# First expert chosen from summed slot values, the second batch's keys and values ahead of W1, one subtraction on GpSimd, and W1's product split in halves

## The chip, the cores and the metric

The kernel runs on one core of a Trainium2 chip. The metric is the device time of one execution in microseconds; the number that counts is the median of three executions.

## The reference

Two layers follow each other. The first is a Linformer-like attention for 8 batches, 8 heads, 576 tokens, head size 64 and 32 memory slots; the second is a mixture of 8 experts in which every token goes to one expert.

```python
a = softmax(phi, axis=2)                        # over the 576 tokens, for each of the 32 slots
k_m = einsum('bhsm,bhsd->bhmd', a, k)           # 32 keys per head
v_m = einsum('bhsm,bhsd->bhmd', a, v)           # 32 values per head
x = softmax(q @ k_m.T / 8) @ v_m                # tokens x (8 heads * 64)
xn, en = x / |x|, expert_emb / |expert_emb|     # router
expert = argmax(xn @ en.T / tau); gate = max(softmax(xn @ en.T / tau))
out = gate * (relu(x @ w1[expert]) @ w2[expert])
```

## The kernel before

**Layout.** The 8 heads are two groups `g` of four, so that 4 heads by 32 slots fill 128 partitions. All matrices are float32. The product with W1 is folded into the values: `project` multiplies the 32 slot values of every head with the head's rows of W1 (tile `pg`), and `first` then multiplies the attention weights of the tokens with that product (tile `ph`). Both operands of `ph` are cut into a rounded part and a rest: `aT[0]` and `aT[1]` for the weights (`part`), `gh` (ScalarE) and `gl` (VectorE) for the product. `ph` has three matmuls per group, of which the third needs `gl`.

**Order.** Nothing is scheduled by the compiler: every engine runs its instructions in the order in which the Python code emits them, and semaphores make it wait for data and for free buffers. PSUM has eight tiles by tag, `m0` to `m3` (taken in turn by `mm`, or by number) and `t0` to `t3` (`pt`). A new tile in a tag waits until the last reader of the old one is done. In particular `pg` of group 0 and the first tile `ph` both lie in `m0`, and `pg` of group 1 and the second `ph` in `m1`; the tile `tv` of the second batch's values and the first tile `tt` of `turned` both lie in `m2`. DMAs of the SP queue have eight completion semaphores in turn, so the ninth waits for the first.

**The start.** The change is in the start of the program alone, up to the first `ph`. It runs through batch 0's softmax over tokens (`softmax`, `turn`, `tails`: exponentials `ex`, transposed into `eT`), the slot sums (`slots`, into `ks`), keys and values (`keys`, `values`: tiles `tk`, `tv`, copied to `kT`, `vT`), the scores (`score`: tiles `tr` and `te`, turned into `x` by `fill`), the softmax over slots (`weigh`: maximum, subtraction, exponential; `divide`: sum, reciprocal, product; `turn`: into `aw`), the attended values and router logits (`attend`: tile `po`, then `best`), and the transposes of `turned` (tile `tt`). The same first steps for batch 1 are interleaved. Every batch's tokens take mainly one expert, whose weights are loaded whole; for batch 0 the kernel guesses this expert early (`guess`, `pick`) so that the load of W1 can start. Before the change the guess sums `vv[:, g, D : D + E]`, the logits of every slot, which `squares` (tile `tl`) and `products` have to make first. `warm` issues matmuls whose results nobody reads.

From the first `ph` on (L759) the TensorE works through `first` and `second` of batch 0, the next batches' steps laid between, to the end.

Of the kernel before, what the change touches and what calls it, by code (L numbers as in the profile page):

```python
# [8 lines left out]
F32 = mybir.dt.float32  # L9
# [4 lines left out]
ALU = mybir.AluOpType  # L14
AX = mybir.AxisListType
# [12 lines left out]
BL = S // 32  # L28
HS = S // 2
# [18 lines left out]
class Tokens:  # L48
# [15 lines left out]
        for g in gs:  # L64
            nc.vector.transpose(k.x[:, g, ks], src[g])

    def weigh(self, gs, ks):
        k, nc, b = self.k, self.nc, self.b
        x = k.x[:, gs[0] : gs[-1] + 1, ks]
        n = len(gs) * (ks.stop - ks.start)  # L70
        mx = k.wk.tile([P, *x.shape[1:3]], F32, tag=f"mx{n}", name=f"mx{b}_{gs[0]}{ks.start}")
        nc.vector.tensor_reduce(out=mx, in_=x, axis=AX.X, op=ALU.max)
        yield
        nc.vector.tensor_tensor(out=x, in0=x, in1=mx.unsqueeze(3).broadcast_to(x.shape), op=ALU.subtract)
        yield
        nc.scalar.activation(x, x, AF.Exp, scale=1.0 / 8.0)

    def divide(self, gs, ks, apart=False):
# [8 lines left out]
        nc.vector.reciprocal(out=z, in_=z)  # L87
        for i in parts:
# [94 lines left out]
    def all_at_once(self):  # L183
# [4 lines left out]
        nc.vector.tensor_reduce(out=key, in_=self.room.rearrange("p (i e) -> p e i", e=E), axis=AX.X, op=ALU.add)  # L188
        return key

    def guess(self):

        k, nc = self.k, self.nc
        key = self.pt([P, 512], "key")
        self.spare, self.key = key[:, E:], key[:, :E]
# [89 lines left out]
class Kernel:  # L285
# [312 lines left out]
    def keys(self, b, room=None):  # L598

        ts = [(room or self.pt)([P, NG, P], f"tk{b}_{g}") for g in range(1 if b else NG)]  # L600
        for g in range(NG):
            self.nc.tensor.transpose(ts[-g][:, g], self.ks[:, g, : 2 * D], self.ident)
        kT = self.kT[b % 2]
        if b > 1:
            self.nc.vector.tensor_copy(kT, ts[0])
        elif b:
            self.nc.scalar.copy(kT, ts[0])
        else:
            self.nc.scalar.copy(kT[:, 0], ts[0][:, 0])
            self.nc.vector.tensor_copy(kT[:, 1], ts[1][:, 1])  # L610

    def by_feature(self, b):

# [114 lines left out]
    def project(self, n, vT, room=None, apart=False):  # L728

        nc = self.nc  # L730
        for k in range(2):
            f = slice(512 * k, 512 * k + 512)
            ps = [(room or self.mm)([P, 512], f"pg{n}_{k}{g}") for g in range(NG)]
            for g, j, r, c, i in self.heads():
                nc.tensor.matmul(ps[g][j], lhsT=vT[r, g, c % 2, i], rhs=self.w1s[r, c, f], start=True, stop=True)
            if apart and not k:
                yield
            for g in range(NG):
                nc.scalar.copy(self.gh[:, g, f], ps[g])  # L739
            if apart and not k:  # L740
                yield
            for g in range(NG):
                nc.vector.tensor_tensor(  # L743
                    out=self.gl[:, g, f], in0=ps[g], in1=self.gh[:, g, f].bitcast(F32), op=ALU.subtract
                )
            yield

# [183 lines left out]
    def batch(self, b, t, u):  # L931
# [150 lines left out]
def moe_linformer(ctx, tc, phiT, qT, kv, kvt, emb, tau, w1, w2, out):  # L1082
    k = Kernel(ctx, tc, phiT, qT, kv, kvt, emb, tau, w1, w2, out)
# [42 lines left out]
    def scores(g):  # L1126
        k.score(0, tr, 64, S, (g,))
        k.score(0, te, 0, 64, (g,))

    scores(0)  # L1130
# [5 lines left out]
    scores(1)
    work = [t.weigh((g,), all) for g in range(NG)]
    t.fill((0,), slice(2, BL), tr)
    t.fill((0,), slice(0, 2), te)
    e = t.pick()  # L1140
# [5 lines left out]
    list(work[0])  # L1146
    for g in range(NG):
        k.largest(1, g)
        k.softmax(1, (g,))
    k.turn(1, 0)  # L1150
    k.warm(2, at=2)
    t.fill((1,), slice(2, BL), tr)
    t.fill((1,), slice(0, 2), te)
    list(work[1])
# [4 lines left out]
    next(project)  # L1159
# [3 lines left out]
    t.divide(range(NG), all, True)  # L1163
    k.invert(1)
    next(project)
    k.scale(1)
    k.again(k.nc.scalar.copy)
    t.turn(range(NG), all)
    next(project)
    k.part(0, slice(0, HS), k.nc.scalar.copy)  # L1170
    k.keys(1, lambda *a: k.mm(*a, 3))
    k.values(1, copy=k.nc.scalar.copy, room=lambda *a: k.mm(*a, 2))
    k.part(1, slice(0, HS), k.nc.scalar.copy)
    k.load_w2(e)
# [37 lines left out]
```

## Time and profile before

| what | value |
|---|---|
| median of 3 runs | 394.56 us (394.25 to 394.57) |
| the profiled execution's own time | 397.13 us |
| its span, first to last instruction | 395.3 us |
| PE busy | 384.2 us, 97% of the span |
| DVE, ACT, POOL busy | 243.5, 213.8, 188.0 us |
| DMA moved | 91.25 MB, mean 231 GB/s |

Busy time is the time in which an engine had an instruction running. The profiled execution took 1.8 us more than its span, and 2.6 us more than the median of the runs.

### The profile page before, as it was taken

To read this page: it belongs to the slowest core of one execution; us is meant where nothing else is said; L and a number is where in the kernel's file an instruction comes from. 1 tells how busy PE (TensorE), PEld (TensorE's weight loads), DVE (VectorE), ACT (ScalarE), POOL (GpSimd) and SP (SyncE) were. 2 spreads that over 40 slices of the span, in tenths; PEclk is the share of its full clock that TensorE was granted. 3 is DMA by queue.
4 is the path that set the end of the run, shared out by engine and by line. 5 is a ranking of instruction groups with operands and counts; after the bars stand their busy time and mean duration, and the time that the engine had idled before them with its cause. 6 is when DMAs were issued, how large, how long until landed. Compare 5 with 4: busy or idle time off the path is not lost. (4 is left out here: it accounts for less than half of the span.)

```text
span 395.3 us, 10409 instructions
## 1 busy us (share of the span) xinstructions
PE 384.2 (97%) x3886; PEld 314.1 (79%) x3886; DVE 243.5 (62%) x799; ACT 213.8 (54%) x666; POOL 188.0 (48%) x231
## 2 busy tenths in 40 slices
PE   8869999999999999999999999999999999999995
PEld 5547978879787987879787897879788897879883
DVE  5485896768872798538971698627961596545000
ACT  5257652868675685657665775667632651145011
POOL 1034971479142951559142971549342781529300
PEclk9989999999999999999999999999999999999999
DMA  7999907898679926997479945997269305890011
GB/s 262 388 335 376 380 29 155 293 384 332 153 218 390 396 80 148 328 375 308 77 167 385 378 163 108 343 373 283 57 158 393 142 2 103 247 397 2 30 53 43
DMA packets 67751, 91.25 MB, mean 231 GB/s; under 512 B 40968, under 2 KB 45576, under 8 KB 67568
## 3 DMA queue, kind: packets, MB, share of 16 engines
q1 hardware_dynamic: 64320, 81.02, 61.5%
q0 software_dynamic: 2688, 8.26, 5.8%
q10 hardware_dynamic: 688, 1.26, 1.1%
q8 instruction: 32, 0.52, 0.6%
q14 instruction: 23, 0.19, 0.2%
HBM read 71.19 MB, written 19.33 MB: 229 GB/s over the span
## 5 line engine op out<-in xcount | busy, mean ns | idle before, releaser
L759 PE MATMUL ph<-aT,gh 128*128 128x288 f32 x512 | 103.1, 297 | 0.0
L799 PE MATMUL py<-wh,hh 128*128 128x512 f32 x256 | 100.9, 394 | 0.0
L799 PE MATMUL py<-wh,hl 128*128 128x512 f32 x256 | 99.9, 390 | 0.0
L799 PE MATMUL py<-wl,hh 128*128 128x512 f32 x256 | 99.9, 390 | 0.0
L725 POOL TENSOR_TENSOR wl<-w2s,wh 128x512 fp32r<-128x512 f32 x64 | 83.1, 1299 | 5.1
L759 PEld LDWEIGHTS ph<-aT,gh 128*128 128x128 f32 x512 | 81.8, 188 | 1.8 <-DVE hl L766 0.8
L759 PE MATMUL ph<-aT,gl 128*128 128x288 f32 x256 | 75.5, 295 | 0.0
L763 ACT ACTIVATE hh<-ph 128x224 fp32r<-128x224 f32 (+1 forms) x128 | 48.8, 388 | 33.7 <-PE ph L759 33.0
L766 DVE SCALAR_TENSOR_TENSOR hl<-ph,hh 128x224 fp32r<-128x224 f32 (+1 forms) x128 | 51.9, 417 | 23.9 <-ACT hh L763 17.2
L804 ACT ACTIVATE ys<-py,gate 128x512 f32<-128x512 f32 (+1 forms) x40 | 25.7, 643 | 62.8 <-PE py L799 33.0
L968 POOL DMA_DIRECT2D out_dram<-ys x28 | 16.2, 580 | 90.0 <-ACT ys L804 89.9
L799 PEld LDWEIGHTS py<-wh,hh 128*128 128x128 f32 x256 | 48.2, 188 | 11.0 <-issue 1.4
L799 PEld LDWEIGHTS py<-wh,hl 128*128 128x128 f32 x256 | 48.1, 188 | 10.1
L799 PEld LDWEIGHTS py<-wl,hh 128*128 128x128 f32 x256 | 48.1, 188 | 9.4
L759 PEld LDWEIGHTS ph<-aT,gl 128*128 128x128 f32 x256 | 48.1, 188 | 0.0
L743 DVE TENSOR_TENSOR gl<-pg,gh 128x512 fp32r<-128x512 f32 x32 | 20.0, 684 | 42.3 <-ACT gh L739 42.3
L715 POOL TENSOR_TENSOR aT<-aw,aT 128x576 fp32r<-128x576 f32 (+1 forms) x18 | 23.5, 1318 | 37.6 <-DVE aT L714 29.3
L724 POOL CAST wh<-w2s 128x512 fp32r<-128x512 f32 x62 | 41.2, 665 | 0.1
L554 ACT COPY eT<-xt 32x256 f32<-32x256 f32 x80 | 32.3, 404 | 1.4
L788 PE MATMUL py<-w2s,h 128*64 128x256 f32 x256 | 29.4, 383 | 0.0
L626 ACT COPY kv<-kt 32x64 f32<-32x64 f32 x96 | 23.3, 243 | 6.4 <-DVE kt L616 5.2
L788 PEld LDWEIGHTS py<-w2s,h 128*64 128x64 f32 x256 | 17.7, 137 | 10.7 <-DVE aw L100 2.1
(176 smaller groups left out, 474.6 us busy)
## 6 DMA issues: line engine op xcount, KB each, us to landing
kx<-kv SPq DMA_DIRECT2D x32, 512.0 KB, 10.4
w2s<-w SPq DMA_DIRECT2D x28, 512.0 KB, 9.9
w1s<-w SPq DMA_DIRECT2D x28, 512.0 KB, 6.3
qt<-qT SPq DMA_DIRECT2D x14, 576.0 KB, 9.1
out_dram<-ys POOLq DMA_DIRECT2D x28, 256.0 KB, 6.3
ad<-aw SPq DMA_DIRECT2D x8, 576.0 KB, 11.1
td<-x SPq DMA_DIRECT2D x56, 72.0 KB, 2.4
ea<-td SPq DMA_DIRECT2D x7, 512.0 KB, 4.2
```

The source lines that it names most:

```text
L554: nc.scalar.copy(eT[to, :8, m].rearrange("p (g k) m -> p g k m", g=NG), xt[at, :, q : BL - 2 : 4])
L626: nc.scalar.copy(y, self.kt[32 * l : 32 * l + 32, g, h + 2 * i :: 2 - 4 * i])
L715: self.nc.gpsimd.tensor_tensor(out=al, in0=a, in1=ah.bitcast(F32), op=ALU.subtract)
L724: (copy or self.nc.scalar.copy)(h, x)
L725: self.nc.gpsimd.tensor_tensor(out=l, in0=x, in1=h.bitcast(F32), op=ALU.subtract)
L743: nc.vector.tensor_tensor(out=self.gl[:, g, f], in0=ps[g], in1=self.gh[:, g, f].bitcast(F32), op=ALU.subtract)
L759: nc.tensor.matmul(p, lhsT=w[:, g, fs], rhs=x[:, g, to], start=g == 0 and k == 0, stop=g == 1 and k == 2)
L763: nc.scalar.activation(self.hh[:, f, at], q, AF.Relu)
L766: nc.vector.scalar_tensor_tensor(out=self.hl[:, f, at], in0=q, scalar=0.0, in1=self.hh[:, f, at].bitcast(F32), op0=ALU.max, op1=ALU.subtract)
L788: nc.tensor.matmul(p[64 * j : 64 * j + 64], lhsT=self.h4[:, f], rhs=self.w2s[:, f, d * j : d * j + d], start=f == 0, stop=f == 7,)
L799: nc.tensor.matmul(p, lhsT=h[:, f, to], rhs=w[:, f], start=f == 0 and k == 0, stop=f == 7 and k == 2)
L804: nc.scalar.activation(y[:, :d], p, AF.Copy, scale=gate[:, i : i + 1])
```

## The change

The key of the first guess is made from the slot sums directly: `summed` multiplies `ks` with `fours` (a column of ones for each head's 32 slots), which gives the sum of the values over slots, and VectorE multiplies it with the embeddings (`ve`); `guess` then sums over partitions. The transposes of the values (`tv`) move behind the first group's scores. On the SP queue all four tiles `kx` of batch 1 stand ahead of W1 (before: three, then W1's first half, then the fourth), and the second half of batch 0's queries goes behind the first half of batch 1's phi. The subtraction of `weigh` for group 0 runs on GpSimd. Batch 1's slot sums move ahead of `project`; `again` for batch 1 moves from ScalarE to GpSimd; `gh` and `gl` of W1's first half are made in column halves, and `gl` moves behind `attend`. The warm matmuls in the middle go from 42 of 168 columns to 26 of 128, and from 2 of 512 columns to 3.

```diff
-    def weigh(self, gs, ks):
+    def weigh(self, gs, ks, v=None):
...
-        nc.vector.tensor_tensor(out=x, in0=x, in1=mx.unsqueeze(3).broadcast_to(x.shape), op=ALU.subtract)
+        (v or nc.vector).tensor_tensor(out=x, in0=x, in1=mx.unsqueeze(3).broadcast_to(x.shape), op=ALU.subtract)
...
+    def summed(self):
+        k, nc = self.k, self.nc
+        self.key = self.pt([P, 512], "key")
+        self.vs = vs = self.key[:, 508:].rearrange("p (g k) -> p g k", g=NG)
+        for g in range(NG):
+            for h in range(2):
+                nc.tensor.matmul(
+                    vs[64 * h : 64 * h + 64, g],
+                    lhsT=k.ks[:, g, D * (1 - h) : D * (2 - h)],
+                    rhs=k.fours[:, h ^ g :: 2],
+                    start=True,
+                    stop=True,
+                )
+        self.ve = k.wk.tile([P, NC, E], F32, tag="ve", name="ve")
+        x = self.ve.rearrange("p (g k) e -> p g k e", g=NG)
+        em = k.vT[1][:, :, 0, D:].rearrange("p g (k e) -> p g k e", e=E)
+        nc.vector.tensor_tensor(out=x, in0=em, in1=vs.unsqueeze(3).broadcast_to(x.shape), op=ALU.mult)
...
-        for g in range(NG):
-            nc.tensor.matmul(self.key, lhsT=k.all1, rhs=k.vv[:, g, D : D + E], start=not g, stop=g == NG - 1)
+        for c in range(NC):
+            nc.tensor.matmul(self.key, lhsT=k.all1, rhs=self.ve[:, c], start=not c, stop=c == NC - 1)
...
-            for g in range(NG):
-                nc.scalar.copy(self.gh[:, g, f], ps[g])
+            n = 2 if apart and not k else 1
+            for j, g in ((j, g) for j in range(n) for g in range(NG)):
+                to, at = slice(512 // n * j, 512 // n * (j + 1)), slice(512 * k + 512 // n * j, 512 * k + 512 // n * (j + 1))
+                nc.scalar.copy(self.gh[:, g, at], ps[g][:, to])
...
-    k.load_q(0)
+    k.load_q(0, (0,))
...
-    k.load_phi(1)
+    k.load_phi(1, (0,))
+    k.load_q(0, (1,))
+    k.load_phi(1, (1,))
...
+    k.load_kv(1)
+    k.keys(0)
+    t.summed()
     k.again()
-    k.load_kv(1, (0, 1, 2))
-    k.keys(0)
-    k.values(0, copy=k.nc.scalar.copy)
...
-    k.load_w1(e, 0)
-    k.load_kv(1, (3,))
-    k.load_w1(e, 1)
-    k.load_q(1, (0,))
-    k.warm(42, hot=t.spare[:, :168])
...
+    k.softmax(1, (0,))
+    list(work[0])
+    k.warm(26, hot=k.mm([P, 128], "warm", 3))
+    k.turn(1, 0)
+    k.softmax(1, (1,))
+    k.warm(3, at=3)
     k.turn(1, 1)
     k.tails(1)
+    list(work[1])
     k.shares(1, v=k.nc.gpsimd, invert=False)
...
     for ks in ((0,), (1,), (4,), (2,), (3,)):
         k.slots(1, accs, ks=ks, first=0 in ks, last=3 in ks)
+    t.divide(range(NG), all, True, lambda: k.invert(1))
...
+    k.scale(1)
+    k.keys(1, lambda *a: k.mm(*a, 3))
+    k.again(k.nc.gpsimd.tensor_copy)
+    values = k.values(1, copy=k.nc.scalar.copy, room=lambda *a: k.mm(*a, 2))
+    next(values)
+    t.turn((0,), all)
+    k.part(0, slice(0, HS), k.nc.scalar.copy)
     next(project)
+    t.turn((1,), all)
     next(project)
     k.part(1, slice(0, HS), k.nc.scalar.copy)
+    t.attend()
+    next(project)
+    list(values)
+    t.turned(0, 1)
+    t.turned(4)
```

On TensorE, between batch 1's slot sums (`acc0t`, `acc`) and the attended values (`po`), the program has this before:

```order
L577 MATMUL acc0t<-kx_73,eT 32x128 x4
L577 MATMUL acc0m<-kx_73,eT 32x128 x4
L602 MATMUL tk_0_544<-ident,ks 128x128 x2
L637 MATMUL tv_0_548<-ident,ks 128x128 x2
L131 MATMUL po_0_569<-vv,aw 64x72
```

And this after:

```order
L601 MATMUL acc0t<-kx_73,eT 32x128 x4
L601 MATMUL acc_469<-kx_73,eT 32x128 x4
L626 MATMUL tk_0_520<-ident,ks 128x128 x2
L661 MATMUL tv_0_525<-ident,ks 128x128 x2
L760 MATMUL pg_00_532<-w1s,kv_80 32x512 x4
L760 MATMUL pg_01_533<-w1s,kv_80 32x512 x4
L133 MATMUL po_0_550<-vv,aw 64x72
```

W1's product `pg`, which stood ahead of all slot sums of batch 1, now stands behind them, between the values and `po`.

On ScalarE, the two exponentials of batch 1's phi (`ex`), the two exponentials of batch 0's scores (`x`) and the copies of the transposes (`eT`, `kt`) stand before in this order:

```order
L76 ACTIVATE x<-x 128x576
L494 ACTIVATE ex,sm_435<-ex,nm_434 128x576 x2
L521 COPY eT<-te_0_443 128x512
L76 ACTIVATE x<-x 128x576
L521 COPY eT<-te_1_458 128x512
L528 COPY kt<-tz_464 128x256
```

And after in this one:

```order
L518 ACTIVATE ex,sm_401<-ex,nm_400 128x576
L76 ACTIVATE x<-x 128x576
L545 COPY eT<-te_0_438 128x512
L518 ACTIVATE ex,sm_401<-ex,nm_400 128x576
L545 COPY eT<-te_1_450 128x512
L552 COPY kt<-tz_456 128x256
L76 ACTIVATE x<-x 128x576
```

Phi's second exponential now stands behind the first copy, and the second exponential of the scores behind all copies.

On VectorE, from the last transposes into `aw` to the rests `gl`, the program has before:

```order
L98 STREAM_TRANSPOSE aw<-x 128x576
L100 STREAM_TRANSPOSE aw<-x 128x64
L743 TENSOR_TENSOR gl<-pg_00_473,gh 128x512
L743 TENSOR_TENSOR gl<-pg_01_474,gh 128x512
L145 TENSOR_REDUCE lg_255<-po_0_569 128x24
```

And after:

```order
L100 STREAM_TRANSPOSE aw<-x 128x576
L102 STREAM_TRANSPOSE aw<-x 128x64
L147 TENSOR_REDUCE lg_257<-po_0_550 128x24
L147 TENSOR_REDUCE l_594<-po_1_551 128x24
L147 TENSOR_REDUCE lg_257<-po_2_552 128x16
L147 TENSOR_REDUCE l_594<-po_3_553 128x16
L148 TENSOR_TENSOR lg_257<-lg_257,l_594 128x40
L156 TENSOR_REDUCE m_260<-lg_257 128x5
L157 TENSOR_TENSOR oh_175<-lg_257,m_260 128x40
L771 TENSOR_TENSOR gl<-pg_00_532,gh 128x256
L771 TENSOR_TENSOR gl<-pg_01_533,gh 128x256
```

The rests `gl` move behind the seven instructions that turn `po` into the choice of experts.

## Rows read from the trace of the kernel before

**Rows 1.** The page, part 1: busy us (share of the span) x instructions, by engine.

```profile
PE 384.2 (97%) x3886; PEld 314.1 (79%) x3886; DVE 243.5 (62%) x799; ACT 213.8 (54%) x666; POOL 188.0 (48%) x231
```

**Rows 2.** Stretches: length, busy us per engine, granted clock, DMA share, GB/s.

```profile
13.00:19.00 6.00, 5.17 (x80) 2.90 (x73) 3.19 (x11) 2.31 (x10) 0.00 (x0) 1.00 1.03 411
19.00:22.00 3.00, 3.00 (x42) 2.99 (x40) 2.96 (x6) 2.31 (x5) 0.29 (x2) 1.00 0.68 222
23.20:26.20 3.00, 0.00 (x0) 0.00 (x0) 2.81 (x7) 1.43 (x3) 1.37 (x5) 0.93 0.97 322
26.20:29.20 3.00, 2.98 (x40) 1.25 (x44) 2.11 (x5) 0.98 (x2) 0.92 (x1) 0.50 1.05 410
...
34.30:391.00 356.70, 356.29 (x3441) 295.06 (x3439) 223.34 (x735) 197.59 (x623) 181.21 (x210) 1.00 0.67 223
```

**Rows 3.** TensorE in order of time: start, length, instruction, what ended idle time.

```profile
14.68 1.06 PE L655 MATMUL tr<-qt,kv 64*32 64x512 f32 x8
...
16.53 0.85 PE L197 MATMUL key<-vv,h 128*128 128x8 f32 x4 [0.47 <-ACT vv L701]
17.32 1.06 PE L655 MATMUL tr<-qt,kv 64*32 64x512 f32 x8
...
18.42 3.22 PE L417 MATMUL key<-ones 128*128 128x168 bf16 x42
21.48 0.60 PE L520 MATMUL te<-ident,ex 128*128 128x128 f32 x4
...
26.22 1.96 PE L735 MATMUL pg<-w1s,kv 64*32 64x512 f32 x16 [3.05 <-DMA w1s<-w]
...
31.60 0.44 PE L602 MATMUL tk<-ident,ks 128*128 128x128 f32 x2 [0.56 <-ACT ks L594]
...
32.30 1.48 PE L131 MATMUL po<-vv,aw 64*64 64x72 f32 x80
...
34.34 0.51 PE L759 MATMUL ph<-aT,gh 128*128 128x288 f32 x2
...
36.10 1.09 PE L735 MATMUL pg<-w1s,kv 64*32 64x512 f32 x16
```

**Rows 4.** ScalarE in order of time, same columns.

```profile
14.78 0.90 ACT L642 COPY kv<-tv 64x64 f32<-64x64 f32 x4 [0.41 <-PE tv L637]
...
20.27 0.78 ACT L494 ACTIVATE ex<-ex,nm 128x576 f32<-128x576 f32 x1
...
22.17 0.59 ACT L521 COPY eT<-te 128x512 f32<-128x512 f32 x1 [0.28 <-PE te L520]
23.21 0.68 ACT L76 ACTIVATE x<-x 128x576 f32<-128x576 f32 x1 [0.45 <-DVE x L74]
...
24.27 0.38 ACT L528 COPY kt<-tz 128x256 f32<-128x256 f32 x1
...
28.22 1.07 ACT L739 CAST gh<-pg 128x512 fp32r<-128x512 f32 x2 [3.58 <-PE pg L735]
```

**Rows 5.** VectorE in order of time, same columns.

```profile
18.76 0.76 DVE L74 TENSOR_TENSOR x<-x,mx 128x576 f32<-128x576 f32 x1
...
28.83 1.29 DVE L743 TENSOR_TENSOR gl<-pg,gh 128x512 fp32r<-128x512 f32 x2 [0.78 <-ACT gh L739]
...
34.18 0.48 DVE L146 TENSOR_TENSOR lg<-lg,l 128x40 f32<-128x40 f32 x1
...
34.93 0.20 DVE L155 TENSOR_TENSOR oh<-lg,m 128x40 bf16<-128x40 f32 x1
...
54.60 1.70 DVE L74 TENSOR_TENSOR x<-x,mx 128x576 f32<-128x576 f32 x1
```

**Rows 6.** GpSimd in order of time, same columns.

```profile
5.49 0.24 POOL L496 COPY xt<-ex 128x64 f32<-128x64 f32 x1 [3.72 <-ACT ex L494]
...
25.48 1.63 POOL L90 TENSOR_TENSOR x<-x,z 128x576 f32<-128x576 f32 x1 [1.45 <-DVE z L87]
...
53.16 2.52 POOL L725 TENSOR_TENSOR wl<-w2s,wh 128x512 fp32r<-128x512 f32 x2
```

More of the change, by code (lines that the diff above doesn't have):

```diff
@@ L73, in weigh, with divide @@
         yield
-        nc.vector.tensor_tensor(out=x, in0=x, in1=mx.unsqueeze(3).broadcast_to(x.shape), op=ALU.subtract)
+        (v or nc.vector).tensor_tensor(out=x, in0=x, in1=mx.unsqueeze(3).broadcast_to(x.shape), op=ALU.subtract)
         yield
         nc.scalar.activation(x, x, AF.Exp, scale=1.0 / 8.0)
-    def divide(self, gs, ks, apart=False):
+    def divide(self, gs, ks, apart=False, then=None):
         k, nc, b = self.k, self.nc, self.b
@@ L87, in divide @@
         nc.vector.reciprocal(out=z, in_=z)
+        if then:
+            then()
         for i in parts:
@@ L189, in all_at_once @@
         return key
+    def summed(self):
[15 more added lines that the diff above has]
+        nc.vector.tensor_tensor(out=x, in0=em, in1=vs.unsqueeze(3).broadcast_to(x.shape), op=ALU.mult)
     def guess(self):
         k, nc = self.k, self.nc
-        key = self.pt([P, 512], "key")
-        self.spare, self.key = key[:, E:], key[:, :E]
-        for g in range(NG):
-            nc.tensor.matmul(self.key, lhsT=k.all1, rhs=k.vv[:, g, D : D + E], start=not g, stop=g == NG - 1)
+        self.key = self.key[:, :E]
+        for c in range(NC):
+            nc.tensor.matmul(self.key, lhsT=k.all1, rhs=self.ve[:, c], start=not c, stop=c == NC - 1)
     def pick(self):
@@ L366, in consts @@
         nc.gpsimd.memset(self.all1, 1.0)
+        self.fours = st([P, 4], F32, name="fours")
+        nc.vector.tensor_reduce(
+            out=self.fours, in_=self.ident.rearrange("p (m x) -> p m x", m=4), axis=AX.X, op=ALU.add
+        )
         self.half = st([P, 1], F32, name="half")
@@ L608, in keys @@
         else:
-            self.nc.scalar.copy(kT[:, 0], ts[0][:, 0])
-            self.nc.vector.tensor_copy(kT[:, 1], ts[1][:, 1])
+            for g in range(NG):
+                self.nc.scalar.copy(kT[:, g], ts[g][:, g])
     def by_feature(self, b):
@@ L737, in project @@
                 yield
-            for g in range(NG):
-                nc.scalar.copy(self.gh[:, g, f], ps[g])
+            n = 2 if apart and not k else 1
+            for j, g in ((j, g) for j in range(n) for g in range(NG)):
+                to, at = slice(512 // n * j, 512 // n * (j + 1)), slice(512 * k + 512 // n * j, 512 * k + 512 // n * (j + 1))
+                nc.scalar.copy(self.gh[:, g, at], ps[g][:, to])
             if apart and not k:
                 yield
-            for g in range(NG):
+            for j, g in ((j, g) for j in range(n) for g in range(NG)):
+                to, at = slice(512 // n * j, 512 // n * (j + 1)), slice(512 * k + 512 // n * j, 512 * k + 512 // n * (j + 1))
                 nc.vector.tensor_tensor(
-                    out=self.gl[:, g, f], in0=ps[g], in1=self.gh[:, g, f].bitcast(F32), op=ALU.subtract
+                    out=self.gl[:, g, at], in0=ps[g][:, to], in1=self.gh[:, g, at].bitcast(F32), op=ALU.subtract
                 )
@@ L1119, in moe_linformer @@
     k.scale(0)
+    k.load_kv(1)
+    k.keys(0)
+    t.summed()
     k.again()
-    k.load_kv(1, (0, 1, 2))
-    k.keys(0)
-    k.values(0, copy=k.nc.scalar.copy)
+    values = k.values(0, copy=k.nc.scalar.copy, room=lambda *a: k.mm(*a, 3))
     all, tr, te = slice(0, BL), [k.mm([P, S - 64], f"tr0_{g}", g) for g in range(NG)], [k.mm([P, 64], "te0_0", 2)]
[L1126 to L1130, printed above, removed]
+    k.score(0, tr, 64, S, (0,))
@@ L1131, in moe_linformer @@
+    t.guess()
+    k.score(0, te, 0, 64, (0,))
+    next(values)
+    t.fill((0,), slice(2, BL), tr)
+    e = t.pick()
+    t.fill((0,), slice(0, 2), te)
+    list(values)
+    k.load_w1(e, 0)
+    k.load_w1(e, 1)
+    k.load_q(1, (0,))
     tl = [k.pt([P, D + E], f"tl0_{g}") for g in range(NG)]
     k.squares(0, tl)
+    k.score(0, tr, 64, S, (1,))
+    te.append(k.pt([P, 64], "te0_1"))
+    k.score(0, te, 0, 64, (1,))
     k.products(0, copy=True)
-    t.guess()
-    te.append(k.pt([P, 64], "te0_1"))
@@ L1136, in moe_linformer @@
[L1136 to L1140, printed above, removed]
-    k.load_w1(e, 0)
-    k.load_kv(1, (3,))
-    k.load_w1(e, 1)
-    k.load_q(1, (0,))
-    k.warm(42, hot=t.spare[:, :168])
-    list(work[0])
+    work = [t.weigh((g,), all, None if g else k.nc.gpsimd) for g in range(NG)]
+    next(work[0])
     for g in range(NG):
         k.largest(1, g)
-        k.softmax(1, (g,))
-    k.turn(1, 0)
-    k.warm(2, at=2)
+    next(work[0])
@@ L1152, in moe_linformer @@
     t.fill((1,), slice(2, BL), tr)
     t.fill((1,), slice(0, 2), te)
-    list(work[1])
+    k.softmax(1, (0,))
[4 more added lines that the diff above has]
+    k.warm(3, at=3)
     k.turn(1, 1)
     k.tails(1)
+    list(work[1])
     k.shares(1, v=k.nc.gpsimd, invert=False)
     project = k.project(0, k.vT[0], apart=True)
-    next(project)
+    accs = [accs[0], k.mm([P, 2 * D], "acc1", 3)]
     for ks in ((0,), (1,), (4,), (2,), (3,)):
@@ L1161, in moe_linformer @@
         k.slots(1, accs, ks=ks, first=0 in ks, last=3 in ks)
+    t.divide(range(NG), all, True, lambda: k.invert(1))
     k.tags, k.turns = 4, 3
-    t.divide(range(NG), all, True)
-    k.invert(1)
+    k.scale(1)
+    k.keys(1, lambda *a: k.mm(*a, 3))
+    k.again(k.nc.gpsimd.tensor_copy)
+    values = k.values(1, copy=k.nc.scalar.copy, room=lambda *a: k.mm(*a, 2))
+    next(values)
+    t.turn((0,), all)
+    k.part(0, slice(0, HS), k.nc.scalar.copy)
     next(project)
-    k.scale(1)
-    k.again(k.nc.scalar.copy)
@@ L1168, in moe_linformer @@
-    t.turn(range(NG), all)
+    t.turn((1,), all)
     next(project)
-    k.part(0, slice(0, HS), k.nc.scalar.copy)
-    k.keys(1, lambda *a: k.mm(*a, 3))
-    k.values(1, copy=k.nc.scalar.copy, room=lambda *a: k.mm(*a, 2))
     k.part(1, slice(0, HS), k.nc.scalar.copy)
+    t.attend()
+    next(project)
+    list(values)
+    t.turned(0, 1)
+    t.turned(4)
     k.load_w2(e)
```

4 lines of the change are left out of this document (1 added, 3 removed).

## The prediction

> **What bounds the kernel now.** I read the page first: TensorE is busy for 97% of the span [rows 1]. The table of stretches then says where it is not: from 34.3 us on, where `ph` starts, it is busy for 356.29 of 356.70 us [rows 2]. Nothing behind 34.3 us waits to be shortened, so the change can only move the moment at which this solid block begins. A start earlier by so much ends the kernel earlier by so much, as long as nothing later runs out of data.
>
> The timeline of TensorE shows what holds that moment back [rows 3]. The last transposes of batch 0's side work start at 21.48 us, and then nothing until 26.22 us, when `pg` starts with 3.05 us of idle time before it, ended by the DMA of W1. Two things come on top. The table of stretches shows the DMA at 411 GB/s up to 19 us but at 222 GB/s from 19 to 22 us: the queue ran dry there, waiting for the expert's choice [rows 2]. And the granted clock, still 0.93 on average over the idle stretch, is 0.50 over 26.2 to 29.2 us, that is 1.2 instead of 2.4 GHz [rows 2]: the first `pg` takes 1.96 us where the second, at full clock, takes 1.09 [rows 3]. From there one thing follows the other: slot sums, `tk` at 31.60, `po` at 32.30, `ph` at 34.34 [rows 3].
>
> **The change part by part.** All times below are moments in the span, to be held against 34.34 for the first `ph`.
>
> *DMA and W1.* Ahead of W1 now stands another tile `kx` of 512 KB, 1.3 us at 411 GB/s. Before, 189 GB/s were lost for 3 us, some 570 KB [rows 2]; that hole closes, since W1 is asked for while the queue is still full. So W1's first half lands about as before, between 25 and 27 us (from 26.22). But `pg` now stands behind the slot sums and values and comes to it only near 29 us (below). W1 is off the path with 2 us to spare, and so is the moment of the guess; the price of the extra tile is nothing, and 1.3 us if that cover were gone. The second half of W1 and W2 keep their order and move the same way.
>
> *Up to the second group's scores.* Batch 0's keys come as before. In place of the two transposes of the values stand eight passes of `key` (four matmuls, two passes each) with 64-column weights. The nearest row is the old `key`: four passes in 0.85 us, a wait in between included [rows 3], so 0.2 us each at most. They hide partly behind the copy of `kT`; I take the first scores `tr` at 14.7 instead of 14.68, at worst 15.4. Behind `tr` (0.9 us from start to the next start) come the new `guess`, eight passes with 128-column weights: between 0.85 (the old four with no wait) and 1.7 us; I take 1.1, since one of the two starts in the old row was a wait. Then the transposes `tv`, their four copies on ScalarE (0.90 us [rows 4]) and `tl`. That puts the second `tr` at 18.1 us, against 17.32 [rows 3]: later by 0.8.
>
> *The warm matmuls.* From `tr` to the warm ones it is 1.1 us (17.32 to 18.42). The old 42 took 3.22 us [rows 3]; 26 of 128 columns instead of 168 are 3.22 x 26/42 x 128/168 = 1.5 us. So the transposes `te` of phi start at 18.1 + 1.1 + 1.5 = 20.7 us, 0.8 earlier than 21.48.
>
> *GpSimd's subtraction.* VectorE's took 0.76 us [rows 5]; the nearest row on GpSimd, a product of the same shape, took 1.63 [rows 6]. It runs beside VectorE's two maxima of phi, from about 18.5 to 20.2 us. The exponential that reads it must be done before the copy of `te` at 21.4, so it is hidden with 0.5 us to spare. What may break this cover is contention: an identical subtraction on VectorE, beside GpSimd's `wl`, took 1.70 instead of 0.76 us [rows 5, 6]; doubled, GpSimd's would take 3.3 and cost 1.1 us. The Trainium skill (GPSIMD Engine Reference, section Specifications) says that the two engines share their SBUF interfaces and get in each other's way when VectorE's instruction reads two tensors from SBUF. Maxima read one, so by that rule the subtraction stays near 1.6 and the sum is as mine; the slow row of 1.70 us agrees, as that subtraction reads two.
>
> *ScalarE's new order.* Here the change costs. `te` at 20.7 gives its copy at 21.4 (0.69 later, as 21.48 to 22.17 [rows 3, 4]), done at 22.0. Only then comes phi's second exponential, 0.78 us [rows 4], with its accumulator about 22.9; then the second `te`, whose copy runs from 23.6 to 24.2, the tail's copy (0.38) to 24.5, and the second exponential of the scores, 0.68 us, to 25.1. Before, that ended at 23.21 + 0.68 = 23.89 [rows 4]. So `weigh` ends 1.2 us later, and it now stands on the path.
>
> *The slot sums* start at about 23.6 and end near 26.3 us, at full clock: no idle stretch of 3 us stands before them any more. They would be done 4 us earlier than before, but their scaling waits for the reciprocals that VectorE makes behind the sums of `divide`.
>
> *From `divide` to `po`.* From the end of that exponential to the end of GpSimd's product it took 27.11 - 23.89 = 3.2 us [rows 4, 6]; the instructions between are the same, so the product ends at 28.3. Behind it on GpSimd stands `again`: 128 columns, where 64 took 0.24 us [rows 6], so between 0.24 and 0.5; I take 0.3. The transposes `tv` wait for it and `pg` waits behind them, so `pg` runs from 28.9 to 29.9 (1.02 to the next start, at full clock), and `po` starts at 29.95, 2.35 us earlier than 32.30. `aw`, ready at 29.3, is in time.
>
> *From `po` to `ph`.* The choice of experts ended 35.13 - 32.30 = 2.8 us after `po` began [rows 3, 5], of which 0.48 was one sum of 40 columns, where the maximum's flags of the same size took 0.20 [rows 5]; I take 2.7, that is 32.65. Only now come the four halves of `gl`. The old two took 1.29 us [rows 5]; a half costs between 0.32 (half of 0.65) and 0.65; I take 0.36. The first `ph` writes to the tag `m0`, which the third half is the last to read, so it starts after three of them, 1.1 us, at 33.75. Before, `gl` was done long ahead; this is 1.1 us given back. ScalarE's four half casts (the old two took 1.07 [rows 4]) and its copies of `tv`, on which `tt` waits, end near 32.7 and hide behind `po` and `gl`.
>
> *The sum.* 34.34 - 33.75 = **0.6 us earlier**. The gain of 2.35 us at `po` comes from the wait for W1 and the halved clock; `gl`, the later start of `po`'s reader and the longer chain on ScalarE give the rest back. The span goes from 395.3 to 394.7 us. The profiled execution was 2.6 us above the median, so I subtract from the median: 394.56 - 0.6 = 394.0 us.
>
> **The rivals.** A run of this kernel varies by 0.3 us, and 0.2%, 0.8 us, is about what can be told from no change; below 393.8 is faster, above 395.35 slower.
>
> *The chain is shorter than I add it up* (18%). The bounds of `guess` (0.25 us down), `gl` (0.1) and the choice of experts (0.2 down, if that sum takes 0.20), and an earlier first copy on ScalarE, together give 0.6 to 1.5 us more: 393.0 us. For it speaks that `po` moves by 2.35 us, against it that all of this lies in series on three engines.
>
> *The clock falls* (15%). This one ends slower. Before, three idle microseconds were followed by the granted clock 0.50 [rows 2]. After the change no gap is that long, but between 22 and 33 us there are idle stretches of 1.0, 0.5, 0.9, 0.9 and 1.3 us by the sums above. If the clock is 0.50 when `pg` and `po` run, `pg` takes 1.96 for 1.09 [rows 3] and `po` up to 2.9 for 1.48: 1.8 to 2.3 us more, against 0.6 gained. The point of decision is whether the clock is at 1.2 GHz at 29 us; time 395.7 us. The Trainium skill (TensorE: Matmul & The Clock Gate, section What's actually happening) says that the slow clock is the default and activity lifts it; sparse work would then cost it, which rows 2 bear out for an empty stretch only.
>
> *Nothing is gained* (12%): the first scores start late (15.4), or the second exponential does by another 0.7 us; then `ph` starts at 34.4 and the time is 394.6 us.
>
> *W1 is late after all:* it would have to land after 28.9 us, 2.7 later than now, with less than 1.3 us of transfer added. I give it nothing of its own.
>
> **How the numbers follow.** My own case has 55%, with 393.4 to 394.6 as its range, a third of it below 393.8. Faster: 0.20 from it and 0.18 from the shorter chain, 0.38. Slower: 0.14 from the clock and 0.03 from the lost gain, 0.17. The same: 0.45. The range reaches from the shorter chain to the slow clock, 392.9 to 395.6 us.
>
> **What the profile will show.** Right: no wait for W1 ahead of `pg`; DMA near 400 GB/s from 19 to 22 us; the second exponential of the scores ending near 25 us; `tv` waiting for GpSimd's `again`; `po` near 30; the first `ph` near 33.75, with a wait for `gl` before it. Wrong: a granted clock of 0.50 behind 26 us; `pg` waiting for a DMA; a subtraction on GpSimd of over 2 us; TensorE idle anywhere behind the first `ph`.

## The result, and the profile after

The changed kernel takes 398.22 us (median of 22 runs, 396.85 to 402.74), the kernel before, run beside it, 396.33 us (22 runs, 393.86 to 399.23). The ratio is 1.0058, with a 95% interval of 1.0033 to 1.0083. I forecast 394.0 us, a gain of 0.6; by the ratio the change costs about 2.3 us (the two medians lie 1.9 us apart).

The profiled execution of the changed kernel took 401.59 us. The stretches of its span (length, busy us of each engine, granted clock, DMA share, GB/s) answer to [rows 2]:

```profile
19.00:22.00 3.00, 2.71 (x29) 1.57 (x30) 2.52 (x6) 2.06 (x9) 1.16 (x1) 0.50 0.80 308
14.20:24.30 10.10, 9.81 (x81) 6.05 (x81) 5.27 (x14) 3.61 (x13) 1.40 (x2) 0.50 0.96 370
...
38.50:395.00 356.50, 356.50 (x3438) 294.87 (x3438) 222.80 (x733) 196.48 (x620) 180.89 (x209) 1.00 0.67 219
```

The second row shows a granted clock of 0.50, that is 1.2 GHz, for 10 us, in the middle of the steps whose lengths I had added up at 2.4 GHz. In the kernel before, it was 0.50 at another place, over 26.2 to 29.2 us [rows 2]. TensorE in order of time, against [rows 3]:

```profile
14.91 1.93 PE L680 MATMUL tr<-qt,kv 64*32 64x512 f32 x8
16.78 1.88 PE L217 MATMUL key<-ve,h 128*128 128x8 f32 x8
...
25.07 0.61 PE L544 MATMUL te<-ident,ex 128*128 128x128 f32 x4
...
33.24 1.09 PE L760 MATMUL pg<-w1s,kv 64*32 64x512 f32 x16
34.26 1.48 PE L133 MATMUL po<-vv,aw 64*64 64x72 f32 x80
36.69 0.87 PE L165 MATMUL tt<-ident,aw 128*128 128x128 f32 x6 [0.94 <-ACT kv L667]
38.42 0.50 PE L787 MATMUL ph<-aT,gh 128*128 128x288 f32 x2 [0.86 <-DVE gl L771]
```

`tr` takes 1.93 us here, where it took 1.06 at full clock, and everything behind it is late: `ph` starts at 38.42 us, not at the 33.75 of the forecast. But this is one execution of 22, slower than the median by 3.4 us, so a bad clock in it alone can't be the reason of the median. Two questions follow: does the chain come out as forecast when the clock stays up, and if it does, why is the kernel slower?

Each run carries the mean granted clock of its span. A run whose profile shows a fall of 3.4 us ahead of the end has 0.995 or less (the profiled execution of before: 0.995). Below, a run is called *clean* when its mean is 0.996 or more. The limit is a rough one: nine of the 54 clean runs of the kernel before stand at 0.996 exactly, with a median of 396.9 us, so some of them may hold a fall.

### The profile page after: what moved, and what is told of

The parts are those of the page before. It is cut to its first block, busy times and chain, and to the rows that moved or that the text cites. A ratio compares the mean times of both kernels' runs of the same rounds, so it can differ in the third digit from the quotient of the medians.

```text
span 399.8 us, 10412 instructions
## 1 busy us (share of the span) xinstructions
PE 387.5 (97%) x3883; PEld 315.1 (79%) x3883; DVE 243.2 (61%) x801; ACT 213.7 (53%) x668; POOL 188.9 (47%) x233
## 3 DMA queue, kind: packets, MB, share of 16 engines
q10 hardware_dynamic: 688, 1.26, 1.1%
## 5 line engine op out<-in xcount | busy, mean ns | idle before, releaser
L771 DVE TENSOR_TENSOR gl<-pg,gh 128x512 fp32r<-128x512 f32 (+1 forms) x34 | 20.1, 651 | 42.8 <-ACT gh L766 42.8
L740 POOL TENSOR_TENSOR aT<-aw,aT 128x576 fp32r<-128x576 f32 (+1 forms) x18 | 23.5, 1318 | 35.9 <-DVE aT L739 29.2
## 6 DMA issues: line engine op xcount, KB each, us to landing
w2s<-w SPq DMA_DIRECT2D x28, 512.0 KB, 10.1
```

What stands on the lines that cost most here:

```text
L740: self.nc.gpsimd.tensor_tensor(out=al, in0=a, in1=ah.bitcast(F32), op=ALU.subtract)
L771: nc.vector.tensor_tensor(out=self.gl[:, g, at], in0=ps[g][:, to], in1=self.gh[:, g, at].bitcast(F32), op=ALU.subtract)
```

## The experiments

Each kernel ran 11 or 12 times beside the kernel before, which ran 35 times beside the first four, 34 beside the next four and 23 beside e9 and e10; e11 and e12 ran once each, on the chip of e9 and e10. The ratio is against these. The three groups ran on three chips, so clean runs are best held against the row of before that ran beside them.

| kernel | median us (runs) | ratio (95%) | clean runs: number, median us | first `ph` in its profile |
|---|---|---|---|---|
| before, beside e1 to e4 | 395.9 (35) | | 22, 394.72 | |
| before, beside e5 to e8 | 396.22 (34) | | 21, 394.67 | |
| before, beside e9 and e10 | 396.31 (23) | | 11, 395.19 | |
| e1 after, unchanged | 397.42 (12) | 1.0045 (1.0014 to 1.0077) | 7, 396.98 | 33.77 |
| e2 four warm | 397.92 (12) | 1.0062 (1.0032 to 1.0092) | 3, 397.65 | 35.58 |
| e3 `gl` first | 396.88 (12) | 1.0039 (1.0005 to 1.0072) | 7, 396.30 | 32.45 |
| e4 `again` on ScalarE | 397.24 (12) | 1.0028 (0.9998 to 1.0058) | 8, 396.72 | 33.86 |
| e5 before, unchanged | 397.07 (12) | 1.0012 (0.9980 to 1.0044) | 4, 394.92 | 33.20 |
| e6 after, gaps filled | 398.86 (11) | 1.0086 (1.0054 to 1.0118) | 9, 398.71 | 33.90 |
| e7 before, gap filled | 396.43 (12) | 1.0018 (0.9989 to 1.0047) | 9, 396.12 | 35.28 |
| e8 e6 + e3 + e4 | 397.12 (12) | 1.0043 (1.0011 to 1.0076) | 9, 396.74 | 32.53 |
| e9 `gl` first, values on VectorE | 395.15 (12) | 0.9990 (0.9963 to 1.0018) | 8, 394.75 | 31.81 |
| e10 e9, ScalarE's old order | 393.99 (12) | 0.9949 (0.9919 to 0.9980) | 9, 393.27 | 30.55 |
| e11 before, one look | 395.42 (1) | | 1, 395.42 | 32.11 |
| e12 before, one look | 395.13 (1) | | 0 | 32.27 |

**e1, the changed kernel again**, for a trace in which the clock stays up.

> The changed kernel once more, to see which state of TensorE's clock is usual in it. Clock theory: the profiled run (401.59 us, clock 0.50 from 14.1 to 24.4 us) is a late recovery that most runs do not have; a run with less time at 0.50 should have its first ph about as much earlier as its stretch from the first tr (14.9 us) to phi's first te (25.07 us) is shorter, with the rest from te to ph unchanged at 13.35 us, and should take 397.5 to 398.5 us. Chain theory (the clock matters little, the serial chain is longer than forecast): the first ph stays behind 36 us even in a run whose clock is 1.00 from 5 to 40 us.

It stayed at 2.4 GHz up to the first `ph`. First two stretches of its span, then TensorE, ScalarE, VectorE and GpSimd in order of time:

```profile
19.00:22.00 3.00, 2.67 (x36) 2.04 (x33) 2.93 (x6) 1.96 (x5) 0.24 (x1) 1.00 1.03 398
...
34.10:37.40 3.30, 3.30 (x20) 2.55 (x26) 1.30 (x10) 1.00 (x3) 0.00 (x0) 0.50 1.08 308
```

```profile
14.07 1.06 PE L680 MATMUL tr<-qt,kv 64*32 64x512 f32 x8
15.06 1.06 PE L217 MATMUL key<-ve,h 128*128 128x8 f32 x8
...
18.95 1.63 PE L441 MATMUL warm<-ones 128*128 128x128 bf16 x26
20.41 0.61 PE L544 MATMUL te<-ident,ex 128*128 128x128 f32 x4
...
28.22 0.44 PE L661 MATMUL tv<-ident,ks 128*128 128x128 f32 x2 [0.86 <-POOL ks L655]
28.59 1.09 PE L760 MATMUL pg<-w1s,kv 64*32 64x512 f32 x16
29.61 1.48 PE L133 MATMUL po<-vv,aw 64*64 64x72 f32 x80
32.03 0.87 PE L165 MATMUL tt<-ident,aw 128*128 128x128 f32 x6 [0.94 <-ACT kv L667]
33.77 0.60 PE L787 MATMUL ph<-aT,gh 128*128 128x288 f32 x2 [0.87 <-DVE gl L771]
```

```profile
24.01 0.70 ACT L76 ACTIVATE x<-x 128x576 f32<-128x576 f32 x1
...
31.11 0.87 ACT L667 COPY kv<-tv 64x64 f32<-64x64 f32 x4
```

```profile
31.49 0.68 DVE L148 TENSOR_TENSOR lg<-lg,l 128x40 f32<-128x40 f32 x1
...
32.43 0.20 DVE L157 TENSOR_TENSOR oh<-lg,m 128x40 bf16<-128x40 f32 x1
32.55 1.41 DVE L771 TENSOR_TENSOR gl<-pg,gh 128x256 fp32r<-128x256 f32 x4
```

```profile
17.83 1.16 POOL L74 TENSOR_TENSOR x<-x,mx 128x576 f32<-128x576 f32 x1 [5.41 <-DVE mx L72]
...
26.30 1.63 POOL L92 TENSOR_TENSOR x<-x,z 128x576 f32<-128x576 f32 x1 [2.13 <-DVE rs L538]
27.88 0.29 POOL L655 COPY ks<-ks 128x128 f32<-128x128 f32 x1
...
31.32 0.79 POOL L740 TENSOR_TENSOR aT<-aw,aT 128x288 fp32r<-128x288 f32 x1 [2.25 <-ACT aT L739]
```

`ph` starts at 33.77 us: the forecast said 33.75. So the chain was added up rightly (that the agreement is so close is luck, see below), and still the clean runs, at 396.98 us, are 2.3 us above the clean runs of before, at 394.72. In this execution the clock fell right behind the first `ph`, over 34.1 to 37.4 us where TensorE was busy all the time; its 398.13 us stand 1.2 us above the clean median.

**e2, more warm matmuls ahead of 14 us.**

```diff
-            k.warm(1)
+            k.warm(4 if ks[0] == 2 else 1)
```

> Three more warm matmuls of 512 columns in the gap in which TensorE waits for the last tile of batch 0's keys and values (12.25 to 12.90 us), 0.64 us at full clock, so nothing is delayed. Clock theory: the fall at 14.15 us comes from the sparse stretch around 12 to 13 us, and the filled gap prevents it in most runs: 1 to 2 us less than the changed kernel, 396.0 to 397.0 us, with the granted clock 1.00 from 10 to 20 us. Chain theory: no difference from the changed kernel (within 0.5 us).

The clock fell all the same, at 18.4 us instead of 14.2, with TensorE busy for the whole of the stretch:

```profile
18.40:21.80 3.40, 3.40 (x35) 2.71 (x28) 2.86 (x6) 1.84 (x5) 1.03 (x2) 0.50 1.02 399
```

Only 3 of 12 runs are clean, and the time expected, 396 to 397 us, was missed. Filling this place doesn't keep the clock up.

**e3, `gl` ahead of `attend`; e4, `again` on ScalarE.** Each undoes one term of the sum.

```diff
-    t.attend()
     next(project)
+    t.attend()
     list(values)
```

> The rests gl of W1's first half go ahead of the seven VectorE instructions that read po (the call of the third step of project before attend, no other change). Chain theory: the 1.1 to 1.4 us that the first ph waits for gl are on the path; VectorE sits idle there while po runs, so the first ph starts 1.0 us earlier against te, and the time is 0.8 to 1.2 us below the changed kernel. Clock theory alone: no difference, since the work between 14 and 25 us is as before.

```diff
-    k.again(k.nc.gpsimd.tensor_copy)
+    k.again(k.nc.scalar.copy)
```

> The copy again of batch 1 by ScalarE, as before the change, instead of behind GpSimd's product. Chain theory: tv no longer waits 0.86 us for GpSimd, pg and po come 0.6 to 0.9 us earlier, but po then waits for the second group's aw (33.5 us in the profiled run), so 0.3 to 0.8 us below the changed kernel. Clock theory alone: no difference.

TensorE in e3:

```profile
29.39 1.48 PE L133 MATMUL po<-vv,aw 64*64 64x72 f32 x80
31.82 0.88 PE L165 MATMUL tt<-ident,aw 128*128 128x128 f32 x6 [0.94 <-ACT kv L667]
32.45 0.51 PE L787 MATMUL ph<-aT,gh 128*128 128x288 f32 x2
```

In e3 `ph` starts 3.06 us behind `po` instead of 4.16 in e1: the order of `gl` cost 1.1 us, as the forecast had it. The clean runs fall to 396.30, by 0.7 only. What is left ahead of `ph` is the wait of `tt`. In e4 `tv` starts 1.10 us behind `tk` instead of 1.30, and the clean runs are 0.26 us faster than e1's: the extra wait for GpSimd is a small term. Neither brings the kernel back to 394.7.

**e5, the kernel before; e6, e7, e8, idle gaps filled with warm matmuls.** e6 fills the changed kernel's gaps:

```diff
-        self.key = self.key[:, :E]
+        self.spare, self.key = self.key[:, E:], self.key[:, :E]
...
+    k.warm(6, hot=t.spare[:, :168])
     tl = [k.pt([P, D + E], f"tl0_{g}") for g in range(NG)]
...
-    k.warm(3, at=3)
+    k.warm(7, at=3)
...
+    k.warm(4, at=0)
     k.scale(1)
     k.keys(1, lambda *a: k.mm(*a, 3))
+    k.warm(3, at=0)
...
+    k.warm(4, at=3)
     list(values)
```

e7 puts `k.warm(12, at=2)` into the wait for W1 of the kernel before (ahead of `k.shares(1, ...)`). e8 is e6 with the edits of e3 and e4 (and two warm matmuls, not four, ahead of `list(values)`).

> The kernel before, unchanged, once more, to see which state of TensorE's clock is usual in it. Clock theory: when the granted clock falls in it, it falls after the empty stretch ahead of W1's product (23 to 26 us), where TensorE waits anyway, or not at all, and no dense work behind the first ph runs at 0.50; the first ph comes at 34.3 us or up to 1.5 us earlier. Chain theory: it varies by as much as the changed kernel and its first ph stays near 34.3 us.

> The changed kernel with warm matmuls in all of its idle stretches: 6 of 168 columns ahead of tl, 7 of 512 instead of 3 between the two te, 4 of 512 ahead of tk, 3 ahead of tv, 4 ahead of tt; by the trace each fills a wait and delays nothing at full clock by over 0.1 us. Clock theory: the fall behind po (0.50 for 3.4 us over the first ph in the second profile) goes away, granted clock 1.00 from 6 us to the end in most runs, and the median falls by 1.0 to 1.7 us from the changed kernel's 397.4, to 395.7 to 396.4. Chain theory: no difference, within 0.4 us, or slower by what the warm matmuls delay.

> The kernel before with 12 warm matmuls of 512 columns (2.6 us at full clock) in the wait for W1. Clock theory: the fall at the end of that wait goes away, pg takes 1.1 instead of 1.96 us and the slot sums run at full clock; up to 1.4 us below the kernel before in runs in which W1 is late, nothing in runs in which the clock stayed up; median 0.3 to 1.0 us lower. If W1 usually lands earlier than in the profile, the warm matmuls delay pg and it is slower by up to 1 us. Chain theory: no difference.

> The changed kernel with the warm matmuls of the run before last (2 instead of 4 ahead of tt), the rests gl ahead of the reading of po, and the copy again on ScalarE. Both theories: the chain loses 1.1 us at gl and up to 0.3 us at tv, and the clock stays up, so the first ph starts at 32.1 to 32.5 us; median 394.8 to 395.4 us, 2.0 to 2.6 us below the changed kernel and 0.5 to 1.2 us below the kernel before.

In e5 the clock fell at 25.5 us, near the place of [rows 2], and again the profiled time, 397.64 us, lies far above its clean runs, 394.92. e6 and e8 show no fall ahead of the end in their traces, and `ph` at 33.90 and 32.53, where e1 and e3 have it without the fillers. Yet the clean runs of e6 are 1.7 us slower than those of e1. So filling the gaps and keeping the clock up doesn't make the changed kernel fast. e7 and e8 missed their ranges too. In e7, for which 0.3 to 1.0 us of gain were expected, the clean runs are 1.45 us slower than those of before; in its trace the clock fell at 15.2 us, and the twelve warm matmuls (2.75 us) then stood in front of `pg`, at 28.54. In e8 the first `ph` came as expected (32.1 to 32.5), the time did not: 397.12 against 394.8 to 395.4. What makes e6 slower still lies behind the first `ph`; the waits of TensorE behind 36 us (waiting instruction, releaser: total, times, longest; *issue* means that the profile shows nothing waited for, *POOLq* is GpSimd's queue) are, in e6 and then in e5:

```profile
PE acc L601 <- issue: 0.5, 1, 0.5
```

```profile
PE py L799 <- POOLq L991: 0.8, 1, 0.8
```

The first stands in the traces of e6, e7 and e8 (at L577 in e7), the kernels with fillers, and in no other; the second kind in e5 and e2 (and 0.2 us of it in e11), so in either kernel. Neither belongs to the change. The stop does not account for all of the 1.7 us; the rest is open.

**e9 to e12.** By now the suspicion was the base of my sum: the profiled execution of before had lost time to the clock that its clean runs had not, and the median of 394.56 lies with the clean runs. e11 and e12 are the kernel before, unchanged, for a trace without that loss. e9 and e10 take out of the changed kernel what then remains. e9 orders the end of the chain like this:

```diff
-    values = k.values(1, copy=k.nc.scalar.copy, room=lambda *a: k.mm(*a, 2))
+    values = k.values(1, copy=k.nc.vector.tensor_copy, room=lambda *a: k.mm(*a, 2))
...
     t.turn((1,), all)
+    list(values)
+    k.part(1, slice(0, HS), k.nc.scalar.copy)
     next(project)
-    k.part(1, slice(0, HS), k.nc.scalar.copy)
-    t.attend()
     next(project)
-    list(values)
+    t.attend()
```

e10 is e9 with `again` on ScalarE and its order of exponentials put back:

```diff
     list(work[0])
+    k.softmax(1, (1,))
     k.warm(26, hot=k.mm([P, 128], "warm", 3))
     k.turn(1, 0)
-    k.softmax(1, (1,))
+    list(work[1])
     k.warm(3, at=3)
     k.turn(1, 1)
     k.tails(1)
-    list(work[1])
```

> The changed kernel with the four halves of gl ahead of the token sums po, and with the copies of the second batch's values made by VectorE while it would wait for gh, instead of by ScalarE behind the casts. Theory A (with the clock at 2.4 GHz all through, both kernels reach po at about the same moment, near 29.5 us; the loss of the change lies wholly between po and ph, where it takes 4.1 us instead of 2.04, 1.1 of them for gl and 0.9 for the wait of tt): po to ph falls to 2.1 to 2.3 us, the first ph stands near 31.6 us (33.8 for the change, 32.45 with gl first alone), the wait ahead of tt is gone, and runs with a granted clock of 1.00 take 394.5 to 394.9 us, level with those of the kernel before (394.5). Theory B (the profiled execution of the kernel before is a fair picture of it, po at 32.3, and the loss comes from behind the first ph): the runs stay at least 1.5 us above those of the kernel before although ph stands 2.7 us earlier than 34.34.

> The kernel of e9, and in addition ScalarE's order put back: both exponentials of phi ahead of the first copy of te, the second exponential of the scores between the two copies, and the copy again by ScalarE. My term for the change's order on ScalarE was 1.2 us. Theory A (that order is a cost on the path): the second exponential of the scores ends near 22.4 us (24.5 to 25.0 in the change), the slot sums end 0.6 to 0.8 us earlier, and po and ph stand 0.7 to 1.2 us earlier than in e9, ph near 30.6 us; runs at a granted clock of 1.00 take 393.4 to 393.9 us, below the kernel before. Theory B (the slot sums or W1 set po, the exponential's end was never on the path): po stays where e9 has it within 0.3 us and so does the time.

> The kernel before, unchanged, for a trace of it in which the granted clock stays 1.00. Theory A: in such a run pg starts near 25 us, takes 1.05 to 1.1 us and not 1.96, po stands near 29.6 and the first ph between 31.4 and 32.2 us, some 2.4 us earlier than the 34.34 of the profiled execution and 2 us earlier than in the change; the time is 394.0 to 395.0 us. If the clock falls again, ph stands 33 us or later and the time is near 397. Theory B: with the clock at 1.00 ph still stands near 33 to 34 us, and the time of 394.5 comes from shorter work behind it.

> The same kernel once more, since the clock falls in more than half of its executions: same expectation as for e11.

e11 had the clock up. Two stretches of its span and TensorE in order of time:

```profile
25.40:32.10 6.70, 6.14 (x186) 4.67 (x187) 3.96 (x13) 3.83 (x12) 2.58 (x3) 1.00 1.03 401
32.10:388.80 356.70, 356.52 (x3441) 294.90 (x3439) 223.61 (x735) 197.43 (x622) 181.16 (x210) 1.00 0.68 225
```

```profile
14.21 1.06 PE L655 MATMUL tr<-qt,kv 64*32 64x512 f32 x8
...
21.02 0.60 PE L520 MATMUL te<-ident,ex 128*128 128x128 f32 x4
...
25.37 1.09 PE L735 MATMUL pg<-w1s,kv 64*32 64x512 f32 x16 [2.67 <-DMA w1s<-w]
29.37 0.44 PE L602 MATMUL tk<-ident,ks 128*128 128x128 f32 x2 [0.56 <-ACT ks L594]
...
30.07 1.48 PE L131 MATMUL po<-vv,aw 64*64 64x72 f32 x80
31.48 0.88 PE L163 MATMUL tt<-ident,aw 128*128 128x128 f32 x6
32.11 0.51 PE L759 MATMUL ph<-aT,gh 128*128 128x288 f32 x2
```

This is the trace that I should have had as a base. `ph` starts at 32.11, not 34.34, and `po` at 30.07, where the changed kernel in e1 has it at 29.61. From `po` to `ph` it takes 2.04 us here, 4.16 in e1. The time, 395.42, was a little over the range given for it.

In e12 the clock fell early, where it fell in the profiled execution of the changed kernel, and, against the expectation, that cost next to nothing; a stretch of its span and TensorE:

```profile
14.70:21.50 6.80, 6.26 (x61) 3.43 (x54) 3.95 (x10) 2.58 (x10) 0.00 (x0) 0.50 0.75 299
```

```profile
23.91 0.60 PE L520 MATMUL te<-ident,ex 128*128 128x128 f32 x4
...
25.53 1.09 PE L735 MATMUL pg<-w1s,kv 64*32 64x512 f32 x16
...
32.27 0.51 PE L759 MATMUL ph<-aT,gh 128*128 128x288 f32 x2
```

`te` is 2.9 us later than in e11, `pg` only 0.16, for it had been waiting for W1: the wait took up the loss. The changed kernel has no such wait, so a fall that began at about the same place (and lasted longer, 10.1 us against 6.8) moved its `ph` to 38.42; the shorter one of e2, 3.4 us, moved it to 35.58.

e9 and e10 bear the explanation out; TensorE in e9, then in e10, then ScalarE and VectorE in e10:

```profile
29.51 1.48 PE L133 MATMUL po<-vv,aw 64*64 64x72 f32 x80
30.92 0.88 PE L165 MATMUL tt<-ident,aw 128*128 128x128 f32 x6
31.81 0.50 PE L787 MATMUL ph<-aT,gh 128*128 128x288 f32 x2
```

```profile
28.25 1.48 PE L133 MATMUL po<-vv,aw 64*64 64x72 f32 x80
29.66 0.88 PE L165 MATMUL tt<-ident,aw 128*128 128x128 f32 x6
30.55 0.50 PE L787 MATMUL ph<-aT,gh 128*128 128x288 f32 x2
```

```profile
21.77 0.69 ACT L76 ACTIVATE x<-x 128x576 f32<-128x576 f32 x1
```

```profile
31.19 0.20 DVE L148 TENSOR_TENSOR lg<-lg,l 128x40 f32<-128x40 f32 x1
```

In e9 both waits between `po` and `ph` are gone; `ph` follows 2.30 us behind `po`, and the time is level with before: ratio 0.9990 (0.9963 to 1.0018), clean runs 394.75 us against 395.19 beside them. In e10 the second exponential of the scores ends at 22.46 us instead of 24.71 (e1), and `po` and `ph` come another 1.26 us earlier than in e9 (1.06 of it up to `tk`, which is the order of the exponentials, and 0.20 from `tk` to `tv`, which is `again`). This kernel beats the kernel before: 393.99 us against 396.31, ratio 0.9949 (0.9919 to 0.9980), and 393.27 against 395.19 for the clean runs. So the rest of the change was worth a gain, which its orders gave away.

That the end follows the first `ph` can be read from the last group of matmuls, in before and then in e9:

```profile
386.92 3.67 PE L788 MATMUL py<-w2s,h 128*64 128x256 f32 x32
```

```profile
384.39 3.67 PE L816 MATMUL py<-w2s,h 128*64 128x256 f32 x32
```

It starts 352.58 us behind the first `ph` in both, and 352.53 to 352.59 in e4, e10 and e12 (353.10 in e11, which has 0.2 us of the wait named above). The loss of the change doesn't lie behind the first `ph`.

## Why the prediction was wrong

**The steps of the chain were right, within half a microsecond each.** At 2.4 GHz, in e1:

| step of the prediction | forecast | e1 |
|---|---|---|
| start of the new `guess` to the next start | 1.1 us | 0.99 |
| warm matmuls | 1.5 us | 1.46 |
| `te` of phi | 20.7 | 20.41 |
| subtraction on GpSimd, hidden | 1.63 us | 1.16 |
| second exponential of the scores ends | 25.1 | 24.71 |
| its end to the end of GpSimd's product | 3.2 us | 3.22 |
| `again` on GpSimd | 0.3 us | 0.29 |
| `pg`, `po` start | 28.9, 29.95 | 28.59, 29.61 |
| choice of experts done | 32.65 | 32.63 |
| first `ph`, waiting for `gl` | 33.75 | 33.77 |

DMA ran at 398 GB/s from 19 to 22 us, as forecast (308 in the profiled execution, where the guess came late), and nothing waited for W1. The subtraction ran beside VectorE's maxima and took 1.16 us, less than the 1.63 forecast.

That 33.77 meets 33.75 so closely is luck: the first `tr` started at 14.07 us and not at 14.7, the second came 3.81 us behind it and not 3.4, and the choice of experts ended 3.02 us behind `po`, not 2.7. The last of these has a cause that I overlooked. The sum of 40 columns (L148), which I had put at 0.2 to 0.48 us, took 0.68 in e1 beside GpSimd's product (31.32 to 32.11 us) and ended 0.06 us behind it; in e4, in the first trace of before and in e11 it ended 0.06 us behind the product as well. In e3, e9 and e10, where no product ran beside it, it took 0.20. The Trainium skill (GPSIMD Engine Reference, section Specifications) names, for the contention of the two engines, VectorE's instructions that read two tensors from SBUF (or run in a two-port mode); these traces agree, with 0.68 us for the sum of two tensors and 0.20 without GpSimd's product, and with 1.16 us for the subtraction beside maxima that read one.

**The step that failed is the last one of the sum**: "The profiled execution was 2.6 us above the median, so I subtract from the median: 394.56 - 0.6 = 394.0 us", and with it "The gain of 2.35 us at `po` comes from the wait for W1 and the halved clock". I took those 2.6 us for an offset that the change leaves alone. For the most part they were time lost ahead of the first `ph`, above all to the halved clock, and the gain was counted from an execution that had lost it to a sum that had not. Against e11, 34.34 us [rows 3] goes down to 32.11: 1.38 because `pg` to `po` took 4.70 us, not 6.08, at full clock, and 0.85 because `pg` started at 25.37, not 26.22; of these 0.47 were there already at the first scores (14.21 and 14.68), the rest is W1 landing earlier. From the right base the change gives 0.46 us at `po` and loses 2.12 from `po` to `ph`: 1.1 for `gl` (e3) and the rest, about 1.0, for `tt`, which waits 0.94 us for ScalarE's copies of `tv`; the first `ph` stands 1.66 us later. The sum had both, `gl` as "1.1 us given back" and the copies as hidden behind `po` and `gl`. They were hidden behind `gl` indeed, but came forward as a wait of their own when `gl` was moved (e3). The 1.2 us on ScalarE were real as well, measured as 1.06 at `tk` (e10).

Had I subtracted from the profiled execution's own time, 397.13 - 0.6 = 396.5 us, I would have been within half a microsecond of e1's clean runs. Of the 4.2 us between the forecast and the median of 398.22, the base is 2.6 and falls of the clock are 0.3 (the six clean runs among the 22 lie at 397.9); the other 1.4 are not settled (0.45 by the clean runs of e1). The clean runs of e1 and of before differ by 2.3 us and the traces of e1 and e11 by 1.66, and the 0.6 between them is not settled. The two traces come from different chips (the clean runs of before beside e11 lie 0.5 us above those beside e1), and W1 lands at varying moments in the kernel before: `pg` starts at 24.85 us in e5, at 25.37 in e11.

**The rivals.** *The clock falls* had the right sign and the wrong account. The clock does fall in the changed kernel, in 16 of the 22 first runs by their mean clock, but in the kernel before it falls too, in 38 of 92 runs, and takes their median from 394.95 to 397.32 us. In the changed kernel it takes 396.98 to 398.03 in e1; in the first 22 runs the six clean ones lie at 397.9 and the others at 398.3, so there the falls move the median by 0.3 us only. The price that it has depends on where it falls: in the kernel before it cost 1.38 us on `pg` and the slot sums and 0.16 ahead of the wait for W1 (e12). The Trainium skill (TensorE: Matmul & The Clock Gate, section What's actually happening) calls the low clock the default, which activity lifts; in the rows here it lasted while TensorE was busy for 9.81 of 10.10 us. Ahead of the fall in e1 TensorE had been busy for 7.61 of 11.70 us (22.0 to 33.7), but in e4 it was busy for the same 7.61 us of the same stretch and the clock stayed up: what brings a fall at one place and not at another is open. *The chain is shorter* and *nothing is gained* start from the same wrong base. And "A run of this kernel varies by 0.3 us" was read from three runs that lay near the clean median; the 92 runs spread over more than 5 us.

"Nothing behind 34.3 us waits to be shortened" holds in most traces; where it doesn't (e5, e2, e6 to e8), the wait is in both kernels.

## What to carry to other kernels

When the profiled execution lies far outside the runs that give the median, find out what it lost before you subtract anything: here the 0.50 in the clock column and the `pg` of 1.96 us beside one of 1.09 said it. Price the kernel before again at full clock, and count a gain from there. A wait is also a cushion: removing the wait for W1 exposed the end of the chain and every loss ahead of it, and the work that had been done in its shadow (`gl`, the copies, the exponentials in their old order) should have stayed early.

## What the runs showed of the hardware

The granted clock falls to 1.2 GHz at places that differ from run to run of the same program (25.5 us in e5, 14.7 in e12, and not ahead of the last matmuls in e11), also over stretches in which TensorE is busy without a pause (e1, e2). In the changed kernel, matmuls put into idle gaps left the first `ph` where it was within 0.13 us (33.90 in e6 against 33.77 in e1, 32.53 in e8 against 32.45 in e3), but in all three traces with them (e6 to e8) TensorE stopped once for 0.4 to 0.5 us some 166 us behind the first `ph` with nothing to wait for that the profile shows; in the other traces it did not. The cause wasn't tried.

A VectorE sum of two tensors that ran beside a product on GpSimd ended 0.06 us behind that product in four traces (0.47 to 0.68 us for 40 columns); without the product it took 0.20 us (e3, e9, e10).
